# Start of an FFT and two-layer MoE kernel: first stores moved to SyncE's queue, a weight chunk loaded in halves, a weight conversion split over two places

## The chip, the cores and the metric

One core of one Trainium2 chip. The time is device microseconds of one execution; three runs of the kernel before stand beside it, and one further execution was profiled. The inputs are drawn at random, and weights arrive as float64 seen as pairs of 32-bit words.

## What is computed

The reference, cut to what matters (both MoE parts have 6016 tokens, model width 256, hidden width 2048):

```python
X = np.fft.fft(np.fft.fft(x, axis=1), axis=2).real      # x: 2 x 3008 x 256
h = X.reshape(6016, 256) @ w_in
g = np.where(h > 0.0, h, np.exp(np.minimum(h, 0.0)) - 1.0)
y = g @ w_out
h = y @ w2_in
g = np.maximum(h, 0.0) + alpha * np.minimum(h, 0.0)
return (g @ w2_out).astype(np.float32)
```

## The kernel before, in words

The transform along the sequence of 3008 = 47 x 64 is done as two small transforms with a trip through memory between them; the transform along the width of 256 is folded into the first weight matrix.

**The beginning** is written out by hand as the list START (L31 to L40), one entry a step, and each engine takes its own instructions in that order. Stage A of the first batch (`stage_a`, L177) multiplies four chunks of x by a 47-point matrix, two calls of `mm` a half; ScalarE copies each result to `uc`. When a chunk is complete, a third of it (group g = 0) is stored to memory by `store_u` (L192); before, that store goes out from ScalarE's own queue. The step ('v', 0, 0, 32) reads the stored group back in another layout, into `vt` (`load_v`, L199). `delta_0` (L229), `stage_b` (L256) and `spread_0` (L237) turn `vt` into `zt`, the tokens of the first block, and `zb`, a correction row. Tokens and weights of the products stand as a high and a low part: ScalarE copies the high part, VectorE or GpSimd subtracts it to get the low one.

**Weights.** `ld` (L289) loads a chunk as raw words, `conv_h` (L334) turns half a chunk to float32: one ScalarE copy with a scale (`conv_y`, L311) and three VectorE steps (`conv_s`, L328, L330, L332), called a half conversion below. Chunks of w_in then go through `w_fold` (L348), which multiplies them by a 256-point cosine matrix on TensorE in float32 (L355), copies the high part on ScalarE (L360) and subtracts on VectorE (L342). It also sends one row of the product to memory from ScalarE's queue (L359), from where `load_an` fetches it. Chunks of w_out go through `w_split` (L369): ScalarE copy (L392), GpSimd subtraction (L393). In START, both w_in chunks 0 and 1 are loaded ahead of stage A, both folds follow the conversions, and both halves of w_out chunk 0 are converted there.

**The ticks.** After START, `tick` (L555) is called once for each token block and 128 hidden columns. A tick t does `gemm1(t)` on TensorE (six matmuls, L434), `pt` and two `ht` on VectorE (L567 to L569; each reads one operand from a PSUM bank), relu and exp on ScalarE (L586, L588), `combine` on VectorE (L539), `split_hi` on ScalarE (L546), `split_lo` on GpSimd (L552), and `gemm2` (twelve matmuls, L450) of an earlier tick; ticks 0, 1 and 2 are special: at tick 1 `combine(0)` and the split of tick 0 come behind the `ht` of tick 1, and `gemm2(0)` comes at the end of tick 2. Later conversions of weights are put into ticks by the list CONV1 (L48), as (tick of the copy, ticks of the three VectorE steps, tick of the split); `at_conv` puts the copy in the middle of a tick and the other steps at its end. Each `gemm1` needs two PSUM banks that an earlier tick's `ht` sets free. The second MoE part follows after 96 such ticks.

**Queues.** SyncE issues loads and stores in the order of the program and waits in it where a store's data is not there yet. `r64` and `load_an` go out from GpSimd. The tile pools reuse a buffer by its tag, so a raw chunk of w_out and its split parts share the buffer wo0 for chunk 0.

Of the kernel before, what the change touches and what calls it, by code (L numbers as in the profile page):

```python
# [28 lines left out]


START = [  # L31
# [3 lines left out]
    ('conv', 'i', 1, 0), ('conv', 'i', 1, 1), ('fold', 0), ('an', 0), ('fold', 1), ('delta',),  # L35
    ('conv', 'o', 0, 0),
    ('alpha',), ('u', 1), ('load', 'o', 1, 1), ('b',), ('conv', 'o', 0, 1), ('split', 'o', 0, 0), ('v', 1, 0, 32), ('load', 'x', 1, 0), ('u', 2),
    ('load', 'i', 1, 2), ('load', 'x', 1, 1), ('load', 'o', 1, 2), ('load', 'x', 1, 2), ('load', 'i', 1, 3), ('load', 'o', 1, 3),
    ('an', 1),
]  # L40
# [5 lines left out]


CONV1 = [  # L48
# [53 lines left out]
def tile_fft_moe_elu_moe_prelu(  # L102
# [21 lines left out]
    nc = tc.nc  # L124
# [52 lines left out]
    def stage_a(b, c, i):  # L177

        if i == 0:
            uc[b, c] = big.tile([96, 8, 256], F32, tag="big", name="uc")  # L180
        for r0 in (4 * i, 4 * i + 2):
            p = mmtile()
            mm(out=p[0:96], lhsT=f47_sb, rhs=xc[b, c][0:96, r0:r0 + 2, :].rearrange("p r j -> p (r j)"),
               start=True, stop=True)
            act(out=uc[b, c][:, r0:r0 + 2, :].rearrange("p r j -> p (r j)"), in_=p[0:96], func=ACTF.Copy)
        if i == 1 and b == 1:
            for g in range(3):
                store_u(b, c, g)
        if i == 1 and b == 0:
            store_u(b, c, 0, nc.scalar)  # L190

    def store_u(b, c, g, eng=nc.sync):  # L192
        eng.dma_start(out=ud[b][g][c * 8:(c + 1) * 8].rearrange("n m j -> m n j"),
                      in_=uc[b, c][g * 32:(g + 1) * 32])


    vt = {}
# [39 lines left out]
    def spread_0():  # L237
        p = mmtile()
        mm(out=p, lhsT=eye[0:8, 1, 0:128], rhs=eye[0:8, 0, :], start=True, stop=True)
        zb[0] = wk.tile([128, 512], F32, tag="zb", name="zb")  # L240
        act(out=zb[0], in_=p, func=ACTF.Copy)
# [14 lines left out]
    def stage_b(b, g):  # L256
# [3 lines left out]
        for q in range(2):  # L260
# [15 lines left out]
            if q == 0 and b == g == 0:  # L276
                release("b", b, g, 0)
                spread_0()
        if bl == LONG:
            hold(("b", b, g, 1), nc.gpsimd.tensor_copy, out=z[:, :, :, BLOCKS[bl][2] - MOVED:BLOCKS[bl][2]], in_=moved.bitcast(F32))  # L280
        if b == g == 0:
# [6 lines left out]

    def ld(kind, layer, c, eng):  # L289

        home, tag = (big, "big") if (kind, layer, c) in wd else (wp, f"w{kind}{c}")
        if kind == "i":
            src = (w_in, w2_in)[layer - 1][:, c * 512:(c + 1) * 512].bitcast(I32).rearrange("(k p) f -> p k f", p=128)
            t = home.tile([128, 2, 1024], I32, tag=tag, name="w64")
        else:
            src = (w_out, w2_out)[layer - 1][c * 512:(c + 1) * 512, :].bitcast(I32).rearrange("(k p) d -> p k d", p=128)
            t = home.tile([128, 4, 512], I32, tag=tag, name="w64")
        eng.dma_start(out=t, in_=src)
        raw[kind, layer, c] = t
        w32[kind, layer, c] = None  # L300

    w32 = {}

# [44 lines left out]
    def w_fold(c):  # L348

        t = w32.pop(("i", 1, c)).rearrange("p (k f) -> p k f", k=2)  # L350
        w = wp.tile([128, 2, 2, 512], F32R, tag=f"wi{c}", name=f"wi{c}")
        for e in (1, 0):
            p = mmtile()
            for k in range(2):
                mm(out=p, lhsT=c256_sb[:, k, e * 128:(e + 1) * 128], rhs=t[:, k, :], start=(k == 0), stop=(k == 1))  # L355
            if e == 1:
                at_ = wk.tile([1, 512], F32, tag="s", name="at", bufs=4)
                act(out=at_, in_=p[0:1, :], func=ACTF.Copy)
# [79 lines left out]
    def gemm2(L, bl, f, first, last, hi, lo):  # L438
# [4 lines left out]
            accs[L, bl] = [[pa.tile([128, 512], F32, tag=f"acc{d}{t}", name=f"acc{d}{t}") for t in range(2)]  # L443
                           for d in range(2)]
        order = [(t, d, i) for t in range(2) for d in range(2) for i in range(3)]
        if (L, bl, f) == (1, 0, 0):
            order.sort(key=lambda k: k[2] == 2)
        for t, d, i in order:
            a, b = PASSES[i]
# [105 lines left out]
    def tick(t, pre, mid, end):  # L555
# [3 lines left out]
        if cur:  # L559
# [5 lines left out]
            st[t] = dict(n=n, f=f, h=ht[:, :, 0:n], e=et[:, :, 0:n])  # L565
            pt = wk.tile([128, 512], F32, tag="s", name="pt", bufs=4)
            stt(out=pt[:, 0:n], in0=zb[bl][:, 0:n], scalar=an_sb[:, f:f + 1], in1=p[0], op0=ALU.mult, op1=ALU.add)  # L567
            tt(out=ht[:, 0, 0:n], in0=pt[:, 0:n], in1=p[1], op=ALU.add)
            tt(out=ht[:, 1, 0:n], in0=pt[:, 0:n], in1=p[1], op=ALU.subtract)  # L569
        if t == 1:  # L570
            combine(0)
            split_hi(0)
            split_lo(0)
        if t - 2 in st and t > 2:
            split_hi(t - 2)
        for fn in mid:
# [166 lines left out]
    with tc.manual_schedule():  # L743
# [9 lines left out]
        for i in range(2):  # L753
# [14 lines left out]
            "split": lambda kind, c, i: w_split(kind, 1, c, i),  # L768
            "c256": lambda: nc.sync.dma_start(out=c256_sb, in_=c256.rearrange("(k p) f -> p k f", p=128)),
            "r64": load_r64,  # L770
        }
        for what, *args in START:
            start[what](*args)
# [165 lines left out]
```

## Time and profile before

| | us |
|---|---|
| three runs | 970.72, 970.82 (median), 970.96 |
| profiled execution, its own time | 970.64 |
| its span, first to last instruction | 968.5 |
| PE busy in the span | 950.2 |
| DVE busy | 730.8 |
| ACT busy | 655.5 |
| POOL busy | 622.3 |

PE is TensorE's matmuls, DVE VectorE, ACT ScalarE, POOL GpSimd, SP SyncE. The profile numbers all instants from the start of the span. Busy shares are means over a start of some 40 us, the first MoE part up to about 475 us, and the second; each has its own limit, so the start has to be read from timelines of its own stretch. The granted clock is a share of 2.4 GHz: 1.00 is that level, 0.50 is 1.2 GHz.

### The profile page before, as it was taken

To read this page: it belongs to the slowest core of one execution; us is meant where nothing else is said; L and a number is where in the kernel's file an instruction comes from. 1 tells how busy PE (TensorE), PEld (TensorE's weight loads), DVE (VectorE), ACT (ScalarE), POOL (GpSimd) and SP (SyncE) were. 2 spreads that over 40 slices of the span, in tenths; PEclk is the share of its full clock that TensorE was granted. 3 is DMA by queue.
4 is the path that set the end of the run, shared out by engine and by line. 5 is a ranking of instruction groups with operands and counts; after the bars stand their busy time and mean duration, and the time that the engine had idled before them with its cause. 6 is when DMAs were issued, how large, how long until landed. Compare 5 with 4: busy or idle time off the path is not lost.

```text
span 968.5 us, 12229 instructions
## 1 busy us (share of the span) xinstructions
PE 950.2 (98%) x4206; PEld 768.7 (79%) x4206; DVE 730.8 (75%) x1045; ACT 655.5 (68%) x925; POOL 622.3 (64%) x497
## 2 busy tenths in 40 slices
PE   9899999999999999999999999999999999999998
PEld 3576667789888877788888888889988888888886
DVE  2799999989999999987867756566657657566564
ACT  5677777776788878898866666565666566565553
POOL 1364567765777879887779756565665574664543
PEclk9999999999999999999999999999999999999999
DMA  8963322302212511121140110010011011001001
GB/s 322 331 213 85 90 77 88 98 1 88 54 53 80 180 44 33 45 87 44 44 153 1 39 44 1 1 72 16 1 44 39 0 44 44 1 2 44 0 1 44
DMA packets 27013, 64.10 MB, mean 66 GB/s; under 512 B 3076, under 2 KB 11524, under 8 KB 24776
## 3 DMA queue, kind: packets, MB, share of 16 engines
q1 hardware_dynamic: 25536, 62.09, 19.2%
q10 hardware_dynamic: 1160, 1.07, 0.4%
q8 instruction: 33, 0.54, 0.2%
q0 software_dynamic: 256, 0.17, 0.1%
q14 instruction: 28, 0.23, 0.1%
HBM read 41.53 MB, written 21.79 MB: 65 GB/s over the span
## 4 chain that ended last, share of the span: by engine, by line
PE 74%; DVE 17%; DMA 4%; issue 3%; ACT 1%; POOL 0%; SPq 0%; DVEq 0%; ACTq 0%
PE acc L450 41%; PE eet L624 13%; PE mmt L624 10%; PE mmt L434 6%; DVE et L539 3%; DVE pt L567 3%; DVE ht L569 3%; DVE et L536 2%; DVE w L332 2%; DVE sg L330 1%; DMA w<-w_in 1%; PE eet L434 1%; DVE sg L328 1%; DMA xc<-x 1%; DMA w<-w_out 1%
## 5 line engine op out<-in xcount | busy, mean ns | idle before, releaser
L450 PE MATMUL acc<-hi,wo 128*128 128x512 f32 (+1 forms) x1536 | 469.2, 387 | 5.4 <-ACT hi L546 2.4
L650 POOL TENSOR_TENSOR lo<-et,hi 128x512 fp32r<-128x512 f32 (+1 forms) x190 | 237.4, 1281 | 180.6 <-ACT hi L644 180.6
L450 PEld LDWEIGHTS acc<-hi,wo 128*128 128x128 f32 x1536 | 288.5, 188 | 62.0 <-ACT hi L546 2.8
L552 POOL TENSOR_TENSOR lo<-et,hi 128x512 fp32r<-128x512 f32 (+1 forms) x192 | 265.9, 1407 | 104.8 <-issue 46.9
L450 PE MATMUL acc<-lo,wo 128*128 128x512 f32 (+1 forms) x768 | 297.4, 388 | 3.1 <-POOL lo L552 3.1
L644 ACT ACTIVATE hi<-et 128x1024 fp32r<-128x1024 f32 (+1 forms) x96 | 100.3, 1045 | 132.1 <-PE acc L450 68.0
L450 PEld LDWEIGHTS acc<-lo,wo 128*128 128x128 f32 x768 | 144.7, 188 | 34.4 <-POOL lo L552 6.8
L586 ACT ACTIVATE et<-ht 128x1024 f32<-128x1024 f32 (+2 forms) x97 | 100.3, 1034 | 70.5 <-DVE ht L569 66.1
L676 DVE TENSOR_TENSOR v<-mmt,p 128x512 f32<-128x512 f32 (+1 forms) x48 | 32.7, 681 | 144.0 <-ACT p L671 143.8
L434 PE MATMUL mmt<-zt,wi 128*128 128x512 f32 (+1 forms) x444 | 117.1, 394 | 2.1 <-DVE ht L569 1.0
L546 ACT ACTIVATE hi<-et 128x1024 fp32r<-128x1024 f32 (+2 forms) x97 | 99.3, 1024 | 9.3 <-DVE et L539 6.6
L434 PEld LDWEIGHTS mmt<-zt,wi 128*128 128x128 f32 x444 | 82.2, 188 | 24.5 <-DVE ht L569 4.1
L539 DVE SCALAR_TENSOR_TENSOR et<-et,ht 128x1024 f32<-128x1024 f32 (+2 forms) x44 | 75.1, 1708 | 1.8 <-POOL lo L552 1.1
L701 ACT ACTIVATE et<-mmt 128x512 f32<-128x512 f32 (+1 forms) x96 | 56.0, 590 | 29.2 <-PE mmt L624 14.6
L536 DVE SCALAR_TENSOR_TENSOR et<-eet,ht 128x512 f32<-128x512 f32 (+1 forms) x106 | 67.2, 675 | 0.0
L704 DVE SCALAR_TENSOR_TENSOR et<-et,oma_sb,eet 128x512 f32<-128x512 f32 (+1 forms) x96 | 66.2, 731 | 0.0
L704 DVE SCALAR_TENSOR_TENSOR et<-et,oma_sb,mmt 128x512 f32<-128x512 f32 (+1 forms) x96 | 66.1, 730 | 0.0
L567 DVE SCALAR_TENSOR_TENSOR pt<-zb,an_sb,mmt 128x512 f32<-128x512 f32 (+1 forms) x73 | 53.3, 730 | 14.9 <-PE mmt L434 14.7
L593 ACT ACTIVATE eet<-et 128x512 f32<-128x512 f32 (+1 forms) x106 | 58.9, 588 | 3.7 <-DVE et L536 2.1
L624 PE MATMUL eet<-xo,wi 128*128 128x512 f32 (+1 forms) x216 | 59.8, 385 | 0.0
L624 PE MATMUL mmt<-xo,wi 128*128 128x512 f32 (+1 forms) x216 | 59.8, 385 | 0.0
L624 PE MATMUL eet<-xo,sx 128*128 128x512 f32 (+1 forms) x216 | 59.7, 384 | 0.0
(120 smaller groups left out, 1302.7 us busy)
## 6 DMA issues: line engine op xcount, KB each, us to landing
w<-w_in SPq DMA_DIRECT2D x8, 1024.0 KB, 6.2
w<-w_out SPq DMA_DIRECT2D x8, 1024.0 KB, 5.0
vt<-ud SPq DMA_DIRECT2D x6, 1024.0 KB
ud<-uc SPq DMA_DIRECT2D x20, 256.0 KB, 4.4
xd<-xs SPq DMA_DIRECT2D x10, 512.0 KB, 3.1
xs<-xd SPq DMA_DIRECT2D x5, 1024.0 KB, 6.7
out_t<-ot SPq DMA_DIRECT2D x16, 256.0 KB, 2.2
xc<-x SPq DMA_DIRECT2D x5, 768.0 KB, 14.4
```

Of the source, the lines that this page charges most:

```text
L434: mm(out=p[:, 0:n], lhsT=lhsT, rhs=rhs, start=(i == 0), stop=(i == len(ops) - 1))
L450: mm(out=accs[L, bl][d][t][:, 0:n], lhsT=w[:, a, o, d * 128:(d + 1) * 128], rhs=(hi, lo)[b][:, t, 0:n], start=(f == first and i == 0), sto ...
L536: stt(out=s["e"][:, i, :], in0=s["x"][i], scalar=-1.0, in1=s["h"][:, i, :], op0=ALU.add, op1=ALU.max)
L539: stt(out=s["e"][:, i], in0=s["e"][:, i], scalar=-1.0, in1=s["h"][:, i], op0=ALU.add, op1=ALU.max)
L546: act(out=s["hi"][:, i, 0:s["n"]], in_=s["e"][:, i], func=ACTF.Copy)
L552: nc.gpsimd.tensor_tensor(out=s["lo"][:, i, 0:n], in0=s["e"][:, i, :], in1=s["hi"][:, i, 0:n].bitcast(F32), op=ALU.subtract)
L567: stt(out=pt[:, 0:n], in0=zb[bl][:, 0:n], scalar=an_sb[:, f:f + 1], in1=p[0], op0=ALU.mult, op1=ALU.add)
L586: act(out=s["e"][:, i], in_=s["h"][:, i], func=ACTF.Relu, scale=-1.0)
L624: mm(out=bank[:, 0:n], lhsT=w[:, a], rhs=x2[b][:, 0:n], start=(first and m == 0), stop=(last and m == 2), skip_group_check=True)
L644: act(out=s["hi"][f][:, :, 0:n], in_=s["g"][f], func=ACTF.Copy)
L650: eng.tensor_tensor(out=s["lo"][f][:, t, 0:n], in0=s["g"][f][:, t], in1=s["hi"][f][:, t, 0:n].bitcast(F32), op=ALU.subtract)
L704: stt(out=o, in0=o, scalar=oma_sb[:, 2 * j + f:2 * j + f + 1], in1=h, op0=ALU.mult, op1=ALU.add)
```

## The change

- The stores of group 0 of stage A go out from SyncE's queue, each behind its own chunk; that of chunk 3 is cut in two by rows.
- w_in chunk 1 is not loaded ahead of stage A but in two halves: the first issued behind the store of chunk 2, the second behind the last store, ahead of the read of `vt`.
- In START, alpha, the stores of group 1 and the load of w_out chunk 1 come ahead of the conversions of w_in chunk 1 (these are SyncE's, whose own order stays), and `fold 0` comes between the two halves of that conversion. `w_fold` takes the first half of the rows for both banks, then the second half for both.
- w_out chunk 0 is loaded into the buffer wo3. Its first half is converted inside `stage_b`, behind `spread_0`; its second half is converted at tick 1 and split at the end of tick 2. The conversions of w_out chunk 1 and w_in chunk 2 come one tick later.
- At tick 1, `combine(0)` and the split of tick 0 come ahead of the two `ht`, behind `pt`. `gemm2` of the first four column groups of the first block takes its products with `lo` last (before, only the first did).

```diff
--- before.py
+++ after.py
@@ -29,12 +29,12 @@
 
 
 START = [
-    ('r64',), ('eye',), ('load', 'i', 1, 0), ('c256',), ('load', 'i', 1, 1),
-    ('a', 0, 0), ('a', 0, 1), ('a', 1, 0), ('a', 1, 1), ('a', 2, 0), ('a', 2, 1), ('conv', 'i', 0, 0), ('conv', 'i', 0, 1), ('a', 3, 0),
-    ('a', 3, 1), ('v', 0, 0, 32), ('load', 'o', 1, 0),
-    ('conv', 'i', 1, 0), ('conv', 'i', 1, 1), ('fold', 0), ('an', 0), ('fold', 1), ('delta',),
-    ('conv', 'o', 0, 0),
-    ('alpha',), ('u', 1), ('load', 'o', 1, 1), ('b',), ('conv', 'o', 0, 1), ('split', 'o', 0, 0), ('v', 1, 0, 32), ('load', 'x', 1, 0), ('u', 2),
+    ('r64',), ('eye',), ('load', 'i', 1, 0), ('c256',),
+    ('a', 0, 0), ('a', 0, 1), ('a', 1, 0), ('a', 1, 1), ('a', 2, 0), ('a', 2, 1), ('half', 1, 0),
+    ('conv', 'i', 0, 0), ('conv', 'i', 0, 1), ('a', 3, 0), ('a', 3, 1), ('half', 1, 1), ('v', 0, 0, 32), ('load', 'o', 1, 0),
+    ('alpha',), ('u', 1), ('load', 'o', 1, 1),
+    ('conv', 'i', 1, 0), ('fold', 0), ('an', 0), ('conv', 'i', 1, 1), ('fold', 1), ('delta',), ('b',),
+    ('split', 'o', 0, 0), ('v', 1, 0, 32), ('load', 'x', 1, 0), ('u', 2),
     ('load', 'i', 1, 2), ('load', 'x', 1, 1), ('load', 'o', 1, 2), ('load', 'x', 1, 2), ('load', 'i', 1, 3), ('load', 'o', 1, 3),
     ('an', 1),
 ]
@@ -46,9 +46,9 @@
 
 
 CONV1 = [
-    (('o', 1, 0), None, (None, None, 1)),
-    (('o', 1, 1), (2, (2, 3, 3), 5), (4, (4, 5, 5), 6)),
-    (('i', 1, 2), (6, (6, 6, 7)), (8, (8, 8, 9))),
+    (('o', 1, 0), None, (1, (1, 1, 1), 2)),
+    (('o', 1, 1), (3, (3, 3, 4), 6), (5, (5, 6, 6), 7)),
+    (('i', 1, 2), (7, (7, 7, 8)), (9, (9, 9, 10))),
     (('i', 1, 3), (10, (10, 10, 12)), (12, (12, 13, 13))),
     (('o', 1, 2), (14, (14, 14, 15), 17), (16, (16, 17, 17), 18)),
     (('o', 1, 3), (18, (18, 20, 20), 21), (21, (21, 21, 22), 22)),
@@ -186,12 +186,15 @@
         if i == 1 and b == 1:
             for g in range(3):
                 store_u(b, c, g)
-        if i == 1 and b == 0:
-            store_u(b, c, 0, nc.scalar)
-
-    def store_u(b, c, g, eng=nc.sync):
-        eng.dma_start(out=ud[b][g][c * 8:(c + 1) * 8].rearrange("n m j -> m n j"),
-                      in_=uc[b, c][g * 32:(g + 1) * 32])
+        if b == 0 and c == 3:
+            store_u(b, c, 0, rows=(4 * i, 4 * i + 4))
+        elif b == 0 and i == 1:
+            store_u(b, c, 0)
+
+    def store_u(b, c, g, rows=(0, 8)):
+        r0, r1 = rows
+        nc.sync.dma_start(out=ud[b][g][c * 8 + r0:c * 8 + r1].rearrange("n m j -> m n j"),
+                          in_=uc[b, c][g * 32:(g + 1) * 32, r0:r1])
 
 
     vt = {}
@@ -276,6 +279,7 @@
             if q == 0 and b == g == 0:
                 release("b", b, g, 0)
                 spread_0()
+                conv_h("o", 1, 0, 0)
         if bl == LONG:
             hold(("b", b, g, 1), nc.gpsimd.tensor_copy, out=z[:, :, :, BLOCKS[bl][2] - MOVED:BLOCKS[bl][2]], in_=moved.bitcast(F32))
         if b == g == 0:
@@ -288,7 +292,7 @@
 
     def ld(kind, layer, c, eng):
 
-        home, tag = (big, "big") if (kind, layer, c) in wd else (wp, f"w{kind}{c}")
+        home, tag = (big, "big") if (kind, layer, c) in wd else (wp, "wo3" if (kind, layer, c) == ("o", 1, 0) else f"w{kind}{c}")
         if kind == "i":
             src = (w_in, w2_in)[layer - 1][:, c * 512:(c + 1) * 512].bitcast(I32).rearrange("(k p) f -> p k f", p=128)
             t = home.tile([128, 2, 1024], I32, tag=tag, name="w64")
@@ -298,6 +302,13 @@
         eng.dma_start(out=t, in_=src)
         raw[kind, layer, c] = t
         w32[kind, layer, c] = None
+
+    def ld_half(c, h):
+        key = ("i", 1, c)
+        if h == 0:
+            raw[key] = wp.tile([128, 2, 1024], I32, tag=f"wi{c}", name="w64")
+            w32[key] = None
+        nc.sync.dma_start(out=raw[key][:, h], in_=w_in[h * 128:(h + 1) * 128, c * 512:(c + 1) * 512].bitcast(I32))
 
     w32 = {}
 
@@ -349,10 +360,12 @@
 
         t = w32.pop(("i", 1, c)).rearrange("p (k f) -> p k f", k=2)
         w = wp.tile([128, 2, 2, 512], F32R, tag=f"wi{c}", name=f"wi{c}")
+        banks = {1: mmtile(), 0: mmtile()}
+        for k in range(2):
+            for e in (1, 0):
+                mm(out=banks[e], lhsT=c256_sb[:, k, e * 128:(e + 1) * 128], rhs=t[:, k, :], start=(k == 0), stop=(k == 1))
         for e in (1, 0):
-            p = mmtile()
-            for k in range(2):
-                mm(out=p, lhsT=c256_sb[:, k, e * 128:(e + 1) * 128], rhs=t[:, k, :], start=(k == 0), stop=(k == 1))
+            p = banks[e]
             if e == 1:
                 at_ = wk.tile([1, 512], F32, tag="s", name="at", bufs=4)
                 act(out=at_, in_=p[0:1, :], func=ACTF.Copy)
@@ -443,7 +456,7 @@
             accs[L, bl] = [[pa.tile([128, 512], F32, tag=f"acc{d}{t}", name=f"acc{d}{t}") for t in range(2)]
                            for d in range(2)]
         order = [(t, d, i) for t in range(2) for d in range(2) for i in range(3)]
-        if (L, bl, f) == (1, 0, 0):
+        if (L, bl) == (1, 0) and f < 4:
             order.sort(key=lambda k: k[2] == 2)
         for t, d, i in order:
             a, b = PASSES[i]
@@ -565,12 +578,12 @@
             st[t] = dict(n=n, f=f, h=ht[:, :, 0:n], e=et[:, :, 0:n])
             pt = wk.tile([128, 512], F32, tag="s", name="pt", bufs=4)
             stt(out=pt[:, 0:n], in0=zb[bl][:, 0:n], scalar=an_sb[:, f:f + 1], in1=p[0], op0=ALU.mult, op1=ALU.add)
+            if t == 1:
+                combine(0)
+                split_hi(0)
+                split_lo(0)
             tt(out=ht[:, 0, 0:n], in0=pt[:, 0:n], in1=p[1], op=ALU.add)
             tt(out=ht[:, 1, 0:n], in0=pt[:, 0:n], in1=p[1], op=ALU.subtract)
-        if t == 1:
-            combine(0)
-            split_hi(0)
-            split_lo(0)
         if t - 2 in st and t > 2:
             split_hi(t - 2)
         for fn in mid:
@@ -768,6 +781,7 @@
             "split": lambda kind, c, i: w_split(kind, 1, c, i),
             "c256": lambda: nc.sync.dma_start(out=c256_sb, in_=c256.rearrange("(k p) f -> p k f", p=128)),
             "r64": load_r64,
+            "half": ld_half,
         }
         for what, *args in START:
             start[what](*args)
```

## Rows read from the trace of the kernel before

**Rows 1.** The chain of waits, 0 to 140 us: start, length, what held it.
```profile
3.77 13.59 DMA w<-w_in
...
20.64 2.67 DMA ud<-uc
...
23.86 8.29 DMA w<-w_out
...
74.22 0.96 PE mmt L434 x3
```

**Rows 2.** Table by stretches: engines' busy time, granted clock, DMA share, GB/s.
```profile
43.42:46.84 3.42, 3.42 (x10) 2.67 (x9) 2.73 (x4) 3.39 (x5) 2.81 (x3) 0.50 1.06 368
53.30:74.20 20.90, 20.87 (x101) 15.94 (x99) 19.88 (x25) 14.01 (x18) 14.17 (x10) 1.00 0.56 183
74.20:94.00 19.80, 19.74 (x71) 13.18 (x72) 18.21 (x21) 16.65 (x22) 9.33 (x7) 1.00 0.33 79
```

**Rows 3.** Timeline of DVE: start, length, instruction, and idle time before it with its releaser.
```profile
17.39 0.43 DVE L328 TENSOR_SCALAR sg<-w 128x512 int32<-128x512 int32 x1 [15.98 <-DMA w<-w_in]
...
24.37 0.69 DVE L332 SCALAR_TENSOR_TENSOR w<-w,sg 128x512 int32<-128x512 int32 x1
...
35.24 0.42 DVE L328 TENSOR_SCALAR sg<-w 128x512 int32<-128x512 int32 x1
35.69 0.69 DVE L330 SCALAR_TENSOR_TENSOR sg<-w,sg 128x512 int32<-128x512 int32 x1
36.49 0.69 DVE L332 SCALAR_TENSOR_TENSOR w<-w,sg 128x512 int32<-128x512 int32 x1
37.10 0.74 DVE L567 SCALAR_TENSOR_TENSOR pt<-zb,an_sb,mmt 128x512 f32<-128x512 f32 x1
...
45.25 1.23 DVE L539 SCALAR_TENSOR_TENSOR et<-et,ht 128x1024 f32<-128x1024 f32 x1 [0.69 <-ACT et L588]
46.39 1.52 DVE L328 TENSOR_SCALAR sg<-w 128x512 int32<-128x512 int32 x1
...
58.45 0.75 DVE L567 SCALAR_TENSOR_TENSOR pt<-zb,an_sb,eet 128x512 f32<-128x512 f32 x1 [0.50 <-PE eet L434]
...
94.00 0.75 DVE L567 SCALAR_TENSOR_TENSOR pt<-zb,an_sb,mmt 128x512 f32<-128x512 f32 x1 [1.21 <-PE mmt L434]
```

**Rows 4.** Timeline of PE, with the idle time before an instruction and its releaser.
```profile
26.08 1.88 PE L355 MATMUL mmt<-w,c_sb 128*128 128x512 f32 x4
28.39 0.27 PE L232 MATMUL mmt<-r_sb,vt 128*8 128x64 f32 x2 [0.44 <-DMA vt<-ud]
...
34.48 0.73 PE L434 MATMUL mmt<-zt,wi 128*128 128x512 f32 x2 [0.69 <-ACT zt L274]
...
42.63 3.13 PE L450 MATMUL acc<-hi,wo 128*128 128x512 f32 x8 [2.37 <-ACT hi L546]
...
52.95 0.50 PE L450 MATMUL acc<-lo,wo 128*128 128x512 f32 x1 [0.56 <-POOL lo L552]
```

**Rows 5.** DMA queues from 4 to 17.36 us: packets, MB, share of the engines.
```profile
DMA packets 1442, 5.48 MB, mean 410 GB/s; under 512 B 149, under 2 KB 647, under 8 KB 1058
...
q10 hardware_dynamic: 309, 0.30, 6.4%
```

**Rows 6.** Timeline of ACT, the same columns.
```profile
20.01 0.60 ACT L185 ACTIVATE uc<-mmt 96x512 f32<-96x512 f32 x1
...
24.14 0.60 ACT L360 ACTIVATE wi<-eet 128x512 fp32r<-128x512 f32 x1
...
32.17 0.68 ACT L311 ACTIVATE w<-w 128x512 f32<-128x512 f32 x1 [3.58 <-DMA w<-w_out]
...
40.51 0.63 ACT L588 ACTIVATE et<-et 128x512 f32<-128x512 f32 x1
```

**Rows 7.** Timeline of POOL, the same columns.
```profile
42.66 2.53 POOL L552 TENSOR_TENSOR lo<-et,hi 128x512 fp32r<-128x512 f32 x2 [3.45 <-ACT hi L546]
45.81 1.81 POOL L393 TENSOR_TENSOR wo<-w,wo 128x512 fp32r<-128x512 f32 x1 [0.61 <-ACT wo L392]
```

## The prediction, made before the changed kernel was run

> **What bounds the kernel now.** The chain of waits comes first: it tells which unit holds the end in each stretch of the start. It runs through the arrival of w_in chunk 0, the last store of stage A, the arrival of w_out chunk 0 [rows 1], later through DVE from 58 to 74 us, through PE from 74.22 [rows 1] to 94.0, then DVE again. The reader should see that no single unit holds the start: it is handed on. The table by stretches says why: between 53.3 and 94 PE has almost no idle time and DVE hardly more [rows 2], so a gain for one alone is held by the other. The two meet at 74.22, where a `gemm1` waits for a bank that `ht` frees. Last come the timelines, for what each engine waited for: DVE starts when w_in lands at 17.39 [rows 3]; PE waits 0.44 us for `vt` at 28.39, 0.69 for the copy of `zt` at 34.48, and 2.37 for the first `hi` at 42.63 [rows 4]. Right behind that gap the granted clock is 0.50 (1.2 GHz) for 3.42 us [rows 2].
>
> **The change part by part.** All instants are of the profiled execution: span 968.5, own time 970.64, 0.18 under the median of 970.82.
>
> **Stores and x.** Up to 17.36 ACT's queue took 0.30 of 5.48 MB at 410 GB/s [rows 5], 0.7 us of DMA time. Behind the loads in one queue, these stores no longer take it, so w_in chunk 0 may land up to 0.7 earlier; the other bound is 0, and I take 0.7, since DMA was full. PE's stage A isn't touched: it is issued without a gap. ACT loses four issues, which lay in its waits for PE: nothing. SP gets five stores, one more than ACT had, and a second load of w_in; it has nothing else to issue between 5 and 23 us. ACT's last copy of stage A ends at 20.61 [rows 6], and can't come more than about 0.1 earlier, as PE makes it; the store behind it took 2.67 us for 256 KB [rows 1]. At half the size I take 0.3 off (its share at 410 GB/s). The read of `vt` is thus issued some 0.5 earlier and lands at 27.9, not 28.39. Its bounds are 27.5 and 29.3: late if the half of w_in and three stores ahead of it drain slowly.
>
> **The second weight chunk.** It must now come behind fold 0 in DVE's order. Fold 0's copies on ACT end at 24.74 [rows 6], as now: PE still ends stage A at the same time. Its last subtraction on DVE then ends near 25.5. Only then comes the second half conversion, which takes 1.9 us (from 35.24 to the end of L332 at 37.18 [rows 3]): it ends at 27.35, where now it ends at 25.06 [rows 3]. The second half of w_in is issued near 20.9, must land by 25.5, and should by about 24. Fold 1 has four matmuls left behind it, 1.88 us [rows 4]: the end goes from 27.96 to 29.2. So `vt` is no longer what is late: PE gets to `delta_0` at 29.1 instead of 28.39. The rest of `stage_b` took 5.4 us from there; with 0.3 for DVE's subtractions of fold 1, on which `spread_0` now waits, PE is through at 34.9. The conversion in front of ACT's copy of `zt`, where ACT waited 3.58 us for w_out [rows 6], is gone from that place, so the copy follows at once: `gemm1(0)` starts at 35.7, 1.2 later than 34.48 [rows 4].
>
> **The second half of w_out.** Now 1.86 us of DVE stand between the low part of `zt` and the first `pt` (35.24 to 37.10 [rows 3]). In the changed kernel they don't: `pt` starts when PE's third matmul is done, near 36.95, against 37.10: 0.15 earlier, with 1.86 us of DVE work still owed. The other buffer lets the first half be split without the second; the next user of wo3 is loaded late, so it costs nothing.
>
> **Tick 1.** `combine(0)` ahead of `ht(1)`: exp of tick 0 ends at 41.14 now [rows 6], then near 40.95. DVE waits some 0.65 for it in two places, ACT's first `hi` ends at 41.6, and PE starts `gemm2(0)` 1.0 earlier than 42.63. PE's gap is 1.1 in place of 2.37, so I expect no fall of the clock behind it. Products with `lo` last take away PE's wait of 0.56 [rows 4].
>
> **The sum** is DVE's ledger up to 94.0, where DVE last waits for PE; up to the next hand-over behind it DVE has no wait, so what stands there reaches the end. First `pt` −0.15; half conversion owed +1.86; new waits for exp +0.65; waits that go because PE is ahead: 0.69, 0.50 and 1.21 [rows 3], −2.40. That is −0.04. The one tick by which CONV1 is put off is paid back by tick 10.
>
> To it comes what DVE and POOL take from each other. L328 takes 0.42 alone, but 1.52 at 46.39 [rows 3], while POOL subtracts from 45.81 to 47.62 [rows 7]; `pt`, which reads PSUM, isn't stretched. That stall of 1.1 is removed: the subtraction now falls under the `pt` and `ht` of tick 3. A new one can arise at tick 1: POOL's two subtractions of tick 0 (2.53 us [rows 7]) begin near 41.6, the first beside `ht(1)`, the second beside the owed conversion. Its bounds are 0 and 1.26. I take the middle, 0.63, as nothing tells which comes first. The Trainium skill (SBUF — State Buffer, Who interferes with whom) says that a VectorE instruction with two SBUF inputs and a GpSimd instruction that reads SBUF exclude each other for the whole instruction, whichever came first; the stretched L328 agrees in kind. By that rule the conversion pays the full 1.26, and the sum would be near 970.75.
>
> Together: −0.04 − 1.10 + 0.63 = −0.5, from 970.64 to 970.1. The ledger alone runs from −1.14 (no new stall) to +1.2 (full new stall, the old one back elsewhere): 969.5 to 971.9.
>
> **Rivals.** (1) *PE sets the start, DVE's fullness is mostly lock time that gives way.* Then what counts is when PE starts its unbroken run: 1.03 earlier at `gemm2(0)`, half of 3.42 us of low clock back (1.71), and 0.56: −3.3, so 967.3. For it: PE hasn't a gap of note in 53.3 to 94 [rows 2]. Against: the meeting at 74.22 is a wait for DVE, whose work up to there isn't less.
>
> (2) *The clock falls at a new place, and it is slower.* Between fold 1's halves PE now idles: the first half ends near 24.95, the second starts at 27.35, a gap of 2.4, as long as the 2.37 behind which the clock fell [rows 2, 4]. It decides if a gap like that one is enough here. Price: half of 3.42 us, 1.7, all of it ahead of `gemm1(0)`; with the full new stall and the old one kept, 1.26 − 0.04 + 1.7 = +2.9, so 973.6; with the stalls as forecast 971.8. Against: PE works densely on both sides of the gap, while before 42.63 it had also idled at 39.
>
> (3) *The one queue drains slowly*: `vt` at 29.3 and the second half of w_in near 26.3 instead of 25.5. Price 0.85: 971.0, the same side as the forecast.
>
> **How the numbers follow.** A measurement of this kernel can tell about 0.2%, 1.9 us: faster is under 968.9, slower over 972.8. The ledger with its bounds, with (3) in it, gets 0.60: within 0.52, faster 0.05, slower 0.03. Rival 1 gets 0.23, all faster. Rival 2 gets 0.17: slower 0.12, within 0.05. Sums: faster 0.28, same 0.57, slower 0.15. The time is the ledger's, 970.1. The range takes in its bounds, rival 1's 967.3 and the milder rival 2 with 0.6 to spare: 967.2 to 972.4.
>
> **What would show it.** Right: `vt` lands before fold 1 ends; fold 1's last matmul near 29.2; `gemm1(0)` near 35.7; first `pt` near 36.95; `gemm2(0)` near 41.6 at full clock; no wait of DVE for PE at the place of 58.45 and 94.0. The sum is wrong if w_in's second half lands behind 25.5, if the clock is 0.50 anywhere before 45, or if DVE's instructions in ticks 1 to 10 are stretched by over 1.3 us more, or less, than before.

## The result, and the profile after

| | before | after |
|---|---|---|
| median of six runs | 970.88 us | 976.91 us |
| their range | 970.70 to 971.25 | 976.53 to 978.72 |
| profiled execution, own time | 970.64 | 976.53 |
| its span | 968.5 | 974.7 |

The ratio is 1.0066, with a 95% interval of 1.0055 to 1.0077: slower by 6.0 us. The forecast of 970.1 and its range, 967.2 to 972.4, both miss it.

Two lines of the page of the kernel after, busy time and the queue that ScalarE's DMAs use, show that little work was added (PE was at 950.2 and DVE at 730.8) and that the stores of stage A left ACT's queue [rows 5]:

```profile
PE 949.3 (97%) x4206; PEld 767.7 (79%) x4206; DVE 732.3 (75%) x1045; ACT 655.8 (67%) x925; POOL 623.3 (64%) x497
...
q10 hardware_dynamic: 72, 0.02, 0.0%
```

The time is lost in the start. DVE's `pt` (one a tick; tick 0 is the first) is 2.1 us late at tick 0 and 6.1 at tick 11. That stays so up to the 96th `pt`, the last of the first MoE part; DVE's timeline, before and then after, has it 5.97 apart:

```profile
469.84 0.75 DVE L567 SCALAR_TENSOR_TENSOR pt<-zb,an_sb,mmt 128x512 f32<-128x512 f32 x1 [0.74 <-PE mmt L434]
```

```profile
475.81 0.75 DVE L580 SCALAR_TENSOR_TENSOR pt<-zb,an_sb,mmt 128x512 f32<-128x512 f32 x1 [0.74 <-PE mmt L447]
```

So two stretches have to be explained: up to the first `pt`, and from there to tick 11.

**Up to the first `pt`.** The chain of waits of the kernel after, 0 to 150 us (start, length, what held it), has the read of the stored tokens in it, and no longer the arrivals of w_in and w_out [rows 1]:

```profile
20.66 2.87 DMA ud<-uc
23.60 8.09 DMA vt<-ud
```

PE's timeline of the kernel after from 24 to 76 us, only the instructions that PE waited for (start, duration, engine, line, instruction; in brackets the idle time ahead and what ended it):

```profile
24.82 1.13 PE L366 MATMUL eet<-w,c_sb 128*128 128x512 f32 x2 [1.39 <-DVE w L343]
28.72 1.12 PE L366 MATMUL eet<-w,c_sb 128*128 128x512 f32 x2 [1.92 <-DVE w L343]
31.83 0.27 PE L235 MATMUL mmt<-r_sb,vt 128*8 128x64 f32 x2 [1.12 <-DMA vt<-ud]
37.91 1.22 PE L447 MATMUL mmt<-zt,wi 128*128 128x512 f32 x3 [0.69 <-ACT zt L277]
43.80 2.12 PE L463 MATMUL acc<-hi,wo 128*128 128x512 f32 x8 [1.23 <-ACT hi L559]
46.69 0.73 PE L463 MATMUL acc<-lo,wo 128*128 128x512 f32 x2 [0.30 <-POOL lo L565]
50.09 0.98 PE L447 MATMUL eet<-zt,wi 128*128 128x512 f32 x3 [0.96 <-DVE ht L586]
51.88 0.97 PE L447 MATMUL eet<-zt,wi 128*128 128x512 f32 x3 [0.82 <-DVE pt L580]
53.74 2.10 PE L463 MATMUL acc<-hi,wo 128*128 128x512 f32 x8 [0.89 <-ACT hi L559]
56.38 0.73 PE L463 MATMUL acc<-lo,wo 128*128 128x512 f32 x2 [0.53 <-POOL lo L565]
57.80 0.73 PE L463 MATMUL acc<-lo,wo 128*128 128x512 f32 x2 [0.69 <-POOL lo L565]
74.36 0.50 PE L463 MATMUL acc<-hi,wo 128*128 128x512 f32 x1 [0.98 <-ACT wo L405]
75.72 0.50 PE L463 MATMUL acc<-hi,wo 128*128 128x512 f32 x1 [0.85 <-POOL wo L406]
```

Against [rows 4]: `delta_0` starts at 31.83 instead of 28.39, and `gemm1(0)` at 37.91 instead of 34.48, 3.43 later. Fold 1 is late too: its second half starts at 28.72. The gap ahead of `gemm2(0)` is 1.23 instead of 2.37, and the stretch behind it runs at full clock (us, then busy us and count of PE, PEld, DVE, ACT, POOL, then granted clock, DMA share, GB/s):

```profile
40.00:50.00 10.00, 7.60 (x34) 5.19 (x32) 9.13 (x14) 6.26 (x9) 3.28 (x3) 1.00 1.03 351
```

**From the first `pt` to tick 11.** Before, PE waits once behind 43 us, for 0.56 at 52.95 [rows 4]. Now it waits six times between 46 and 58, for DVE at 50.09 (0.96) and 51.88 (0.82) among them, and again at 74.36 and 75.72 for `wo`, a converted half of w_out chunk 1. That is the first time that `gemm2` needs it. DVE's timeline of the kernel after shows where DVE waits, and three stretched conversion steps (45.52, 55.11, 56.64):

```profile
17.20 0.43 DVE L339 TENSOR_SCALAR sg<-w 128x512 int32<-128x512 int32 x1 [15.78 <-DMA w<-w_in]
...
22.82 0.43 DVE L339 TENSOR_SCALAR sg<-w 128x512 int32<-128x512 int32 x1 [1.79 <-DMA w<-w_in]
...
39.17 0.75 DVE L580 SCALAR_TENSOR_TENSOR pt<-zb,an_sb,mmt 128x512 f32<-128x512 f32 x1 [0.59 <-PE mmt L447]
...
43.26 0.69 DVE L552 SCALAR_TENSOR_TENSOR et<-et,ht 128x512 f32<-128x512 f32 x1 [0.49 <-ACT et L601]
...
45.52 1.67 DVE L341 SCALAR_TENSOR_TENSOR sg<-w,sg 128x512 int32<-128x512 int32 x1
...
55.11 1.50 DVE L339 TENSOR_SCALAR sg<-w 128x512 int32<-128x512 int32 x1
56.64 1.65 DVE L341 SCALAR_TENSOR_TENSOR sg<-w,sg 128x512 int32<-128x512 int32 x1
...
62.84 0.75 DVE L580 SCALAR_TENSOR_TENSOR pt<-zb,an_sb,eet 128x512 f32<-128x512 f32 x1 [0.49 <-PE eet L447]
...
80.97 0.75 DVE L580 SCALAR_TENSOR_TENSOR pt<-zb,an_sb,mmt 128x512 f32<-128x512 f32 x1 [0.30 <-PE mmt L447]
...
86.79 0.75 DVE L580 SCALAR_TENSOR_TENSOR pt<-zb,an_sb,mmt 128x512 f32<-128x512 f32 x1 [0.78 <-PE mmt L447]
...
100.11 0.75 DVE L580 SCALAR_TENSOR_TENSOR pt<-zb,an_sb,mmt 128x512 f32<-128x512 f32 x1 [1.74 <-PE mmt L447]
```

100.11 is tick 11, the place of 94.00 [rows 3]. The waits for PE that were to go are still there, and longer.

### The profile page after: what moved, and what is told of

Its sections match the earlier page's. It is cut to its first block, busy times and chain, and to the rows that moved or that the text cites. A ratio compares the mean times of both kernels' runs of the same rounds, so it can differ in the third digit from the quotient of the medians.

```text
span 974.7 us, 12236 instructions
## 1 busy us (share of the span) xinstructions
PE 949.3 (97%) x4206; PEld 767.7 (79%) x4206; DVE 732.3 (75%) x1045; ACT 655.8 (67%) x925; POOL 623.3 (64%) x497
## 4 chain that ended last, share of the span: by engine, by line
PE 76%; DVE 17%; issue 3%; ACT 2%; DMA 1%; POOL 0%; DVEq 0%; ACTq 0%; SPq 0%
PE acc L463 41%; PE eet L637 13%; PE mmt L637 10%; PE mmt L447 6%; DVE et L552 3%; DVE pt L580 3%; DVE ht L586 3%; DVE et L549 2%; DVE w L343 1%; DVE sg L341 1%; PE eet L447 1%; PE eet L183 1%; PE mmt L183 1%; DVE sg L339 1%; DMA vt<-ud 1%
```

## The experiments

The theory after this reading: the start loses to **two late things**, the read of `vt` and fold 1 (theory "two late things"); the ticks lose to **a due time**, the conversions of w_out chunk 1 that come a tick later while `gemm2(4)`, which uses them at the end of tick 7, does not. Rivals: the late read alone; stores in SyncE's queue; POOL's order of subtractions; the half conversion that the change puts among the ticks. To compare kernels I read two instants of each, the start of `gemm1(0)` and of the 96th `pt`; the second less the first is called the ticks' stretch. It is 435.36 before and 437.90 after. The runs of the kernel before that stand beside the experiments have medians of 970.57 (those whose names begin with a), 970.75 (b, c) and 970.78 (d).

### The conversions back to their ticks (a_conv_back)

```diff
-    (('o', 1, 1), (3, (3, 3, 4), 6), (5, (5, 6, 6), 7)),
-    (('i', 1, 2), (7, (7, 7, 8)), (9, (9, 9, 10))),
+    (('o', 1, 1), (2, (2, 3, 3), 5), (4, (4, 5, 5), 6)),
+    (('i', 1, 2), (6, (6, 6, 7)), (8, (8, 8, 9))),
```

> The changed kernel with CONV1's rows of w_out chunk 1 and w_in chunk 2 back at the ticks of before. Theory 'due time': in the changed kernel the split of w_out chunk 1 comes one tick later while the gemm2 that reads it stays where it was, and PE waited 0.98 + 0.85 us there; both waits go, PE isn't late there any more, and the time falls by about 1.8 us to 975.1. Rival 'only the read': everything lost is lost before the first gemm1 (37.91 against 34.48) and merely travels; then the waits were the shadow of a late DVE, the time stays within 0.7 us of 976.9. Rival 'conversions collide': with the conversions a tick earlier DVE and POOL exclude each other more in ticks 2 to 5, and the time rises by 1 us or more.

974.61 (974.33 to 975.40); ratio 1.0042 [1.0027, 1.0057]. PE's timeline at `gemm2(4)` has no wait left:

```profile
70.85 1.95 PE L447 MATMUL mmt<-zt,wi 128*128 128x512 f32 x6
72.64 0.62 PE L463 MATMUL acc<-hi,wo 128*128 128x512 f32 x2
```

The ticks' stretch is 436.33, 1.57 shorter than after's. The due time is shown. Only 1.6 of the 2.3 us between the medians belongs to it: the start, whose code is the same, took 0.86 less in this execution, as the read was issued 0.38 earlier and took 7.6 us instead of 8.09.

### The read ahead of the half (a_read_first)

```diff
-    ('half', 1, 1), ('v', 0, 0, 32),
+    ('v', 0, 0, 32), ('half', 1, 1),
```

> The changed kernel with the read of vt issued ahead of w_in's second half chunk. The read took 8.09 us from issue to landing, 4.93 before. Theory 'queue order': the 512 KB half ahead of it in the same queue holds it; with the read first it takes 5 to 5.5 us and lands near 28.7, but the half then lands some 2.5 us later than now, fold 1 ends no earlier than about 31, and the time moves by less than 1 us from 976.9. Rival 'slow packets': stores of 1 KB pieces and what comes behind slow the queue for all; the read still takes over 7 us, wherever it stands.

981.88 (980.80 to 982.29); 1.0114 [1.0098, 1.0129]. The read, issued at 23.32, moved its last data at 28.0 (27.9 in the kernel before), but now the half was late: issued at 23.71, it took 6.1 us. Fold 1's second half waited for it (PE's timeline), and the granted clock fell to 0.50 (1.2 GHz) within that gap (the stretches):

```profile
31.86 2.07 PE L366 MATMUL eet<-w,c_sb 128*128 128x512 f32 x2 [5.40 <-DVE w L343]
```

```profile
29.75:36.58 6.83, 4.71 (x10) 1.97 (x11) 2.77 (x5) 2.45 (x4) 0.34 (x1) 0.50 1.00 327
```

`gemm1(0)` starts at 42.09. So what stands first in the queue makes the other late, either way round; that the half would be that late I had not expected.

### Both halves early (a_halves_early), and the stores back in ScalarE's queue (a_act_stores)

The first issues both halves of w_in chunk 1 behind the cosine matrix, with the stores still in SyncE's queue; the second gives the five stores to ScalarE again, so that the halves go out early too.

```diff
+    ('c256',), ('half', 1, 0), ('half', 1, 1),
...
```

```diff
-            store_u(b, c, 0)
+            store_u(b, c, 0, eng=nc.scalar)
...
```

> The changed kernel with both halves of w_in chunk 1 issued ahead of stage A, where the whole chunk was before; the stores stay in SyncE's queue behind them. Theory 'queue order': nothing stands ahead of the read but stores; it takes about 5 us, lands near 28.7; w_in chunk 1 is there by 21, fold 1 ends near 29.2, the first gemm1 starts near 35.9 in place of 37.91, and the time falls by about 2 us to 974.9. Rival 'slow packets': the read still takes over 7 us, time within 0.7 us of 976.9. Against both: stores behind 1 MB more in one queue could land later than 23.5, which would show as a later issue of the read.

> The changed kernel with stage A's five stores of group 0 back on ScalarE's queue, the halves of w_in where the change puts them. SyncE then issues the first half at about 5 us (nothing ahead of it waits) and the second right behind, so w_in chunk 1 comes early again. Theory 'queue order': the read takes about 5 us, lands near 28.4, fold 1 ends near 29.2, time about 974.9, as with both halves early. Rival 'two queues share': if the stores on their own queue matter by themselves, the last store lands before 23.3 and the time is a further 0.5 us or more lower than with both halves early in one queue.

977.04 (976.08 to 978.69), 1.0062 [1.0045, 1.0079]; and 976.08 (974.45 to 977.31), 1.0055 [1.0040, 1.0070]. The read took 4.9 and 4.7 us, as it was to, yet fold 1 held the start. PE's timeline of a_act_stores:

```profile
27.83 1.13 PE L366 MATMUL eet<-w,c_sb 128*128 128x512 f32 x2 [2.73 <-DVE w L343]
...
36.30 1.22 PE L447 MATMUL mmt<-zt,wi 128*128 128x512 f32 x3 [0.69 <-ACT zt L277]
```

In a_halves_early PE waited for x in stage A (0.50 and 0.79) and the read was issued only at 24.39. The same gap was 2.85, the clock fell behind it to 0.50 for 3.41 us, and `gemm1(0)` started at 38.23, no earlier than in after. The expectations left out fold 1's order. The runs of the two spread by 2.6 and 2.9 us, and the medians don't tell them from after. Of the instants, those of a_act_stores do, in one execution, the fastest of its four: with the read mended and the clock at 1.00 in the start, `gemm1(0)` is 1.6 earlier than after's, not 3.4.

### The split a tick later (b_split_later)

From a_conv_back, with the split of the second half of w_out chunk 0 at the end of tick 3 instead of 2.

```diff
-    (('o', 1, 0), None, (1, (1, 1, 1), 2)),
+    (('o', 1, 0), None, (1, (1, 1, 1), 3)),
```

> The run with CONV1's rows put back (974.61), with the split of the second half of w_out chunk 0 at the end of tick 3 instead of tick 2. Theory 'POOL order': at tick 2 that split's subtraction stands in POOL's queue ahead of the low part of tick 1 (lo(1) started at 54.05 in the changed kernel), gemm2(1) waits for it, and PE loses 1.2 us from there on; behind lo(1) the waits of PE for POOL in gemm2(1) (0.51 and 0.96) fall below 0.5 in all, and the time falls by about 1.0 to 973.6. Rival 'ledger': VectorE has the same work in either order and sets the pace, PE's waits come back at gemm2(2) or 3; time within 0.4 of 974.6.

974.98 (974.27 to 975.78); 1.0041 [1.0026, 1.0056]. The ticks' stretch is 436.60 against 436.33: nothing gained. POOL's order is not the cause; b_both below, against b_fold_order, says the same (436.70 against 436.55). The start, whose code is that of after and a_conv_back, went another way here: behind a gap of 1.91 us in fold 1 (PE's timeline) the clock was 0.50 for 3.41 us (the stretch).

```profile
28.60 1.83 PE L366 MATMUL eet<-w,c_sb 128*128 128x512 f32 x2 [1.91 <-DVE w L343]
```

```profile
28.88:32.29 3.41, 3.41 (x7) 0.92 (x7) 0.32 (x1) 1.31 (x3) 0.09 (x1) 0.50 0.91 307
```

`gemm1(0)` starts at 38.25, 1.2 later than in a_conv_back, though the read took only 7.1 us.

### Fold 0 behind both half conversions (b_fold_order), with the later split too (b_both)

From a_act_stores, with CONV1 as in a_conv_back and the order of the start as below; b_both adds the later split.

```diff
-    ('conv', 'i', 1, 0), ('fold', 0), ('an', 0), ('conv', 'i', 1, 1), ('fold', 1),
+    ('conv', 'i', 1, 0), ('conv', 'i', 1, 1), ('fold', 0), ('an', 0), ('fold', 1),
```

> CONV1's rows put back, the stores of group 0 on ScalarE's queue and with it both halves of w_in early, and both half conversions of w_in chunk 1 ahead of fold 0, as in the kernel before. Theory 'two late things': fold 0's subtractions ahead of the second conversion held fold 1 (gap of PE 2.73 at 27.83 in the run with the stores on ScalarE's queue) even when the read was early; without it fold 1 ends near 27.6, the read near 28.3 is what PE waits for, the first gemm1 starts near 34.8, and the time is 36.3 - 34.8 = 1.5 under the run with only stores and CONV1 rows undone, which would be 976.1 - 2.3 = 973.8: about 972.3. Rival 'the order of folds is free': the first gemm1 stays at 36 or later, time 973.5 or more.

> The two runs above together: of the change remain the other buffer of w_out, its two halves, the tick 1 order, lo last, the fold's order of rows and the last store in two. If start, due time and POOL's order explain the loss, the first gemm1 starts near 34.8, PE has no wait over 0.6 in gemm2(1) or gemm2(4), and the time is 971.2, within 0.3% of the kernel before; by the ledger in the prediction up to 0.5 below 970.6. Rival 'the half conversion among the ticks costs by itself': 972.3 or more, with DVE's instructions of ticks 1 to 3 stretched.

971.48 (971.32 to 971.94), 1.0007 [0.9998, 1.0017]; and 971.54 (971.09 to 971.93), 1.0006 [0.9996, 1.0015]. PE's timeline of b_fold_order has no wait in fold 1, and `gemm1(0)` is where it was before:

```profile
28.34 0.27 PE L235 MATMUL mmt<-r_sb,vt 128*8 128x64 f32 x2 [1.17 <-DMA vt<-ud]
...
34.43 1.23 PE L447 MATMUL mmt<-zt,wi 128*128 128x512 f32 x3 [0.69 <-ACT zt L277]
...
40.31 2.12 PE L463 MATMUL acc<-hi,wo 128*128 128x512 f32 x8 [1.25 <-ACT hi L559]
...
46.60 0.97 PE L447 MATMUL eet<-zt,wi 128*128 128x512 f32 x3 [0.95 <-DVE ht L586]
48.73 0.96 PE L447 MATMUL eet<-zt,wi 128*128 128x512 f32 x3 [1.16 <-DVE pt L580]
50.25 3.15 PE L463 MATMUL acc<-hi,wo 128*128 128x512 f32 x8 [0.55 <-ACT hi L559]
...
54.58 0.74 PE L463 MATMUL acc<-lo,wo 128*128 128x512 f32 x2 [0.32 <-POOL lo L565]
```

Read and fold together account for the start: 37.91 to 34.43. What stays is in the ticks: `gemm2(0)` starts 2.3 us earlier than before's 42.63 [rows 4], and four waits between 46 and 55 take it back. (The eight matmuls at 50.25 took 3.15 us, at a clock of 0.50; that is hidden, since d_one_queue, at full clock there, takes as long from tick 0 to tick 11: 59.34 against 59.35.)

### Tick 1 alone (c_tick1)

The kernel before, with `combine(0)` and the split of tick 0 ahead of `ht(1)`, and `lo` last in the first four column groups; nothing else of the change.

```diff
-        if (L, bl, f) == (1, 0, 0):
+        if (L, bl) == (1, 0) and f < 4:
...
+            if t == 1:
+                combine(0)
+                split_hi(0)
+                split_lo(0)
...
```

> The kernel before with only two parts of the change: combine(0) and the split of tick 0 ahead of ht of tick 1, and lo last for the first four column groups. Prediction's theory: PE starts gemm2(0) about 1 us earlier, its gap falls from 2.37 to about 1.2, the clock doesn't fall behind it, and DVE's waits for PE at 58.45 and 94.0 shrink; VectorE's ledger gains at most 0.7 + 0.5, so 969.4 to 970.6. Theory 'PE sets the start': the earlier gemm2(0) and the clock are worth 2 us or more, 968.6 or less. Rival 'nothing': both travel into waits, within 0.3 of 970.6.

970.34 (970.23 to 970.66); 0.9994 [0.9985, 1.0003]: a difference that this measurement doesn't resolve. PE's timeline:

```profile
41.82 2.11 PE L450 MATMUL acc<-hi,wo 128*128 128x512 f32 x8 [1.47 <-ACT hi L546]
...
48.76 0.96 PE L434 MATMUL eet<-zt,wi 128*128 128x512 f32 x3 [0.97 <-DVE pt L567]
...
53.06 0.72 PE L450 MATMUL acc<-lo,wo 128*128 128x512 f32 x2 [1.03 <-POOL lo L552]
```

`gemm2(0)` starts 0.81 earlier at full clock (2.11 us for eight matmuls, 3.13 before), and by 53.06 all of it is gone in two waits; before, PE waits for the same `lo` until 52.95 [rows 4].

### The fold's order alone (d_fold_only)

From a_conv_back, with only the order of b_fold_order.

> The changed kernel with CONV1's rows put back and both half conversions of w_in chunk 1 ahead of fold 0; stores and halves stay in SyncE's queue as the change has them. Theory 'one hides the other': the late read (landing near 31) and the fold's order each hold PE; undoing the order alone leaves the read, the first gemm1 stays within 0.7 of 37.05 and the time within 0.7 of 974.6. Rival 'the order is the whole of it': the first gemm1 comes to about 35 and the time to 972.5.

976.08 (975.73 to 976.60); 1.0053 [1.0038, 1.0068]. `gemm1(0)` starts at 37.40, held by the read: mending the fold alone gains nothing there, as the theory has it. But DVE's timeline shows a new wait:

```profile
40.93 0.75 DVE L580 SCALAR_TENSOR_TENSOR pt<-zb,an_sb,mmt 128x512 f32<-128x512 f32 x1 [2.85 <-DMA an_sb<-ad]
```

Fold 0 also sends the row that `an_sb` is loaded from. Behind the second half conversion it goes out later (at 27.57, against 23.68 in a_conv_back), and the first `pt` waits for it. I had not counted that, and the time is outside what the theory allowed (within 0.7 of 974.6).

### One queue, halves early, fold order mended (d_one_queue)

b_fold_order with the stores in SyncE's queue, and both halves issued ahead of them.

> As the run with CONV1's rows, the folds' order and ScalarE's queue (971.48), but with the stores of group 0 in SyncE's queue behind both halves of w_in, which are issued early: the price of one queue by itself. Theory 'the half in front': only the half of w_in between the last store and the read held the read; with the stores in one queue and no load among them the read lands within 0.5 of 28, the first gemm1 within 0.5 of 34.4, time 971.0 to 972.0. Rival 'stores in one queue are late': the last store lands later behind the loads, the read is issued near 24.4 instead of 23.4 (as in the run with both halves early), the first gemm1 near 35.4, time 972.5.

971.70 (971.33 to 971.99); 1.0009 [0.9999, 1.0018]. SyncE's queue issues the read at 23.28, and the view of its line says 4.8 us to landing:

```profile
17.13 3.74 SPq L196 DMA_DIRECT2D ud<-uc  x3
23.28 0.34 SPq L206 DMA_DIRECT2D vt<-ud  x1
```

`gemm1(0)` is at 34.32. Stores ahead of the read in its queue cost nothing; the 512 KB half between them and the read did, as a_read_first shows too.

### The second half of w_out back in the start (d_second_half)

b_fold_order, with that half converted in START again.

```diff
+    ('b',), ('conv', 'o', 0, 1),
...
-    (('o', 1, 0), None, (1, (1, 1, 1), 2)),
+    (('o', 1, 0), None, (None, None, 1)),
```

> As the run with CONV1's rows, the folds' order and ScalarE's queue (971.48), with the second half of w_out chunk 0 converted in START again, behind stage_b, and split at the end of tick 1. From the first gemm1 to the last pt of the first part it took 435.4 us in the kernel before and 436.6 there. Theory 'the half among the ticks costs': that stretch falls by about 1.1 to 435.5 and the time to 970.4. Rival 'tick 1 order or lo last costs': the stretch stays at 436.6, time 971.5; the run of these two parts alone (435.4) speaks against it.

970.77 (970.49 to 971.28); 0.9999 [0.9990, 1.0008], and 0.7 us under b_fold_order (beside nearly equal runs of before). The 96th `pt` starts at 470.09 (b_fold_order: 470.98) from the same `gemm1(0)` (34.48 and 34.43):

```profile
470.09 0.75 DVE L580 SCALAR_TENSOR_TENSOR pt<-zb,an_sb,mmt 128x512 f32<-128x512 f32 x1 [0.74 <-PE mmt L447]
```

The half conversion among the ticks costs 0.9.

### A read in two pieces (d_read_two)

Meant to beat both kernels: c_tick1, with the fold's new row order, and the read cut so that its first three quarters don't wait for the last store.

```diff
-    ('v', 0, 0, 32),
+    ('v', 0, 0, 24), ('v', 0, 24, 32),
```

> A version meant to beat both: the kernel before with the tick 1 order and lo last (970.34), the fold's order of rows, and the read of vt in two pieces, three quarters as soon as the first three stores have landed (near 22), the last quarter behind the last store. If what holds the start is the time from the last store to the landing of 1 MB, the last quarter lands about 2 us earlier than 28.4, w_out chunk 0 about as much, PE gets to delta near 27.3 (end of fold 1), the first gemm1 starts near 33.4 and the time is about 969.2. Rival 'DVE holds it': delta comes earlier but the first pt stays within 0.4 of 37.1, time 970.0 to 970.7.

974.23 (973.27 to 976.18); 1.0037 [1.0023, 1.0051]. The first piece, issued at 22.23, took 6.1 us though it was shorter. What PE waited for is the second, of 256 KB, which landed at 29.53. The chain of waits, PE's timeline, then the stretches:

```profile
23.67 5.86 DMA vt<-ud
```

```profile
29.66 0.27 PE L232 MATMUL mmt<-r_sb,vt 128*8 128x64 f32 x2 [2.40 <-DMA vt<-ud]
...
37.34 0.73 PE L436 MATMUL mmt<-zt,wi 128*128 128x512 f32 x2 [0.69 <-ACT zt L274]
```

```profile
30.27:33.68 3.41, 3.41 (x17) 3.19 (x17) 1.72 (x4) 0.80 (x2) 0.00 (x0) 0.50 1.09 371
```

The first piece was also issued while the last store was on its way (20.97 to 23.65). No run separates that from the cut itself.

No kernel here was shown to be faster than the one before.

## Why the prediction was wrong, point by point

**The sum.** The prediction counted along DVE up to 94.0. Put beside what the two timelines show, term by term (waits are those that the timeline lists behind the first `pt`; the stretch is what conversion steps and full-width `combine`s take beyond their undisturbed 0.42, 0.69 and 1.22 us; the owed conversion stands at its undisturbed 1.86 in each column):

| term of DVE's ledger, us | predicted | after | b_fold_order |
|---|---|---|---|
| first `pt` | −0.15 | +2.07 | −1.41 |
| half conversion owed | +1.86 | +1.86 | +1.86 |
| waits (before: 0.69 + 0.50 + 1.21) | −1.75 | +1.40 | +0.08 |
| DVE and POOL in each other's way | −0.47 | +0.72 | +0.67 |
| sum | −0.51 | +6.05 | +1.20 |
| measured at tick 11 | | +6.11 | +1.04 |

The ledger was a sound frame: with the measured terms it closes to 0.2 us, and what stands at tick 11 reached the end, as the prediction had it. Three of its four terms were mis-sized.

- **"The read of `vt` is thus issued some 0.5 earlier and lands at 27.9", with bounds of 27.5 and 29.3: the step that failed first.** It was issued at 23.60, no earlier than before, as the last store took 2.87 us at half the size (2.67 before), and it landed at 31.69. Half of w_in was priced as one of the things "ahead of it" that might drain slowly, 0.85 at most (rival 3). That was right in kind, and the size was off: 8.09, 7.6, 7.1 and 7.8 us in four executions with this order (after, a_conv_back, b_split_later, d_fold_only), 4.7 to 4.9 without the half. a_read_first, where only the order of the two differs, and d_one_queue, where the stores stay ahead of the read, show that it is the half.
- **Fold 1, "from 27.96 to 29.2".** Its second half started at 28.72, and its last matmuls ended at 30.70. One part is w_in's first half, for which DVE waited until 22.82: the prediction asked when the second half lands, and gave the first no time. Where the halves were early and the read in time (a_act_stores), `gemm1(0)` came at 36.30; the prediction had 35.7. So the order of the fold alone cost 1.8 where 1.2 was forecast, and the read lay on top of it. The two hide each other: against after, mending the read gives 1.6, mending the fold 0.5 at most, both 3.5.
- **"The one tick by which CONV1 is put off is paid back by tick 10".** Wrong, and not worked out: the prediction looked at the work and not at when its product is used. The copy for w_out chunk 1 comes at 73.68 and POOL's split behind it, and `gemm2(4)` waits 0.98 and 0.85 for them. Price 1.6 (a_conv_back).
- **"Waits that go because PE is ahead: 0.69, 0.50 and 1.21".** Not even in b_fold_order, where PE *is* ahead at `gemm2(0)`, by 2.3 us. PE gives that back at 46.60 and 48.73, where it waits for DVE instructions that stand behind the owed conversion, and for `hi` and `lo` behind them (a wait like the second of the two, 0.97 at 48.76, is in c_tick1 too, which owes no conversion); then DVE finds PE no earlier at tick 11. Between two engines that wait for each other, a lead of one can't be booked against the work of the other. The owed half conversion was to cost nothing net; it costs 0.9 at the 96th `pt`, and 0.7 in the medians. Of the 0.9, 0.3 is there at tick 11 (95.04 and 94.73); what adds the rest I did not trace.
- **The stall between DVE and POOL.** The stretch that was to go, L328's 1.52 at 46.39 [rows 3], came back as two steps in a row, 1.50 and 1.65 at 55.11 and 56.64, while POOL subtracts. The new stall came as well: the owed conversion's second step took 1.67 for 0.69 at 45.52, 0.98 more, where the forecast took 0.63 of at most 1.26. So the case was the prediction's outer one, "the old one back elsewhere" with a new one; the row of the table, +0.72, sums over all steps up to tick 11. (L328, the prediction's example, reads one tile; this step reads two, and both are stretched.)
- **w_in chunk 0, "I take 0.7":** it landed 0.2 earlier (17.20 for 17.39), and in d_fold_only, whose stores also stand in SyncE's queue, 0.5 later (17.93). No gain is shown.
- **Right:** the gap at `gemm2(0)` is 1.23 (predicted 1.1) with no fall of the clock; the stores out of ACT's queue and the issues on SyncE cost nothing that these runs resolve (971.70 for 971.48).
- **Rival 1** (PE sets the start, −3.3) falls by c_tick1: `gemm2(0)` 0.81 earlier, with the low clock behind it gone, is worth 0.4 (up to 1.5 by the interval). **Rival 2**, a fall of the clock in fold 1's gap, did not come in the profiled execution of after (gap 1.92), but did in b_split_later, whose start is the same code (1.91), and in a_halves_early (2.85). The ending on the slower side was given 0.15, 0.12 of it for the clock; the 6.0 us of the profiled execution come from the queue, the fold, the due time and the half conversion, at full clock.

**Where the 6.0 us went**, in the profiled executions: 3.4 in the start (read and fold 1 together), 1.6 in the due time of w_out chunk 1, 0.9 in the half conversion among the ticks; together 5.9 of the 5.97 at the 96th `pt`. The parts of the change that could have gained, the queue and tick 1, showed no gain that these runs resolve.

## What to carry to other kernels

When a load is moved ahead of something urgent in a queue, don't price the delay by the load's bytes alone (1.2 us here; it was 2.2 to 3.4), and look which order of the two hurts less; here both orders made `gemm1(0)` over 3 us late, and with the load issued much earlier and the fold's order mended it was on time. When a schedule of producers is put off, list for each product the first consumer and its time before calling it free. And an engine's lead is worth something only if the work that it next waits for is earlier too.

## What the runs showed of the hardware that was not expected

- A 512 KB load ahead in the same queue took the 1 MB read from 4.7 to 4.9 us to between 7.1 and 8.1, more than the 1.2 us that 512 KB take at the 410 GB/s of [rows 5]. In the 8.09 us of after's read the DMA engines moved 267 GB/s, about 2.2 MB, where the read and the whole half are 1.6 MB. An estimate from these numbers is that some 0.6 MB of what was issued behind the read, w_out chunk 0 above all, was moved before the read had landed. What held its last pieces back is open.
- Cutting the read in two didn't make it earlier: 6.1 us for three quarters and 5.9 for the last quarter (d_read_two), 4.9 for the whole. Whether the cut or the store that was still on its way did it is open.
- Gaps of PE of similar length did not end alike. Ahead of fold 1's second half, the clock was 0.50 for 3.41 us behind 1.91 (b_split_later) and 2.85 us, and 1.00 behind 1.90 (a_conv_back), 1.92 (after) and 2.73 (a_act_stores, where it fell later, at 50.09, for 6.83 us). Behind 2.40 (d_read_two) it was 0.50, and within 5.40 (a_read_first) it fell for 6.83.
- In a_halves_early and a_read_first, where CONV1 is after's, the clock also fell for 3.41 us, from 76.39 and from 80.95, right behind the two waits at `gemm2(4)`. Their ticks' stretches are 439.66 and 439.48, 1.6 to 1.8 over after's, about half of 3.41. So the due time could cost more than the 1.6 of a_conv_back; that the fall is the whole of the difference was not tested.
- The kernels with a late read or fold, after among them, spread by 0.9 to 2.9 us from run to run, the other five by 0.4 to 0.8. Of after's six runs the fastest has a mean granted clock of 0.999, the slowest (978.72) of 0.994.
